# Batches 2 and 3 of the attention: two overlapped hand-written schedules replaced by one schedule per batch, with one load buffer instead of two

## The chip, the cores and the metric

One core of one Trainium2 chip. The time is the device time of the whole kernel in microseconds (us), one launch, median of several runs. The profile is one execution of the kernel, recorded by the hardware; its times count from the start of its span.

## What is computed

```python
def phi(x):                                   # per head: 8 x 8 products of two sketches
    a = einsum('rd,bhsd->bhsr', S1, x)
    b = einsum('rd,bhsd->bhsr', S2, x)
    return einsum('bhsi,bhsj->bhsij', a, b).reshape(..., 64)

q_p, k_p = phi(q), phi(k)                     # q, k, v: 4 batches, 4 heads, 1088 tokens, 32 wide
kv  = einsum('bhsf,bhsd->bhfd', k_p, v)
z   = sum(k_p, axis=2)
num = einsum('bhsf,bhfd->bhsd', q_p, kv)
den = einsum('bhsf,bhf->bhs', q_p, z)[..., None] + 1e-6
x   = (num / den) as (4352 tokens, 128)
out = ((1 / (1 + exp(-(x @ w_gate)))) * (x @ w_val)) @ w_out     # 128 -> 1536 -> 128
```

The weights and S1, S2 come in 64-bit floats, the rest in 32-bit floats.

## The kernel before, in words

Two pieces of work are interleaved by hand. The order of the instructions on TensorE, VectorE, ScalarE and GpSimd is the order in which the code emits them; only SyncE's queue of transfers is ordered by the framework.

**The feed-forward part is a row of slots.** The 4352 tokens are cut into eight chunks of 512 and one of 256, and the 1536 hidden columns into twelve groups of 128. A chunk has twelve slots (the last, of 256 tokens, has six); slot 0 to 11 are chunk 0, 12 to 23 chunk 1, 24 to 35 chunk 2, and so on to slot 101. In each slot `w1` emits the matmuls of one group into a PSUM tile `wave` (two buffers, line 542), ScalarE takes the sigmoid of one half (`sg`, line 550), and VectorE multiplies the halves into `g` (`glu`, line 585), which also frees the `wave` buffer for the slot after the next. In chunks 1 to 7 the product with `w_out` is done with seven instead of eight block products; GpSimd forms the sums of tokens for it (`tsum`, line 371), and TensorE's products (`prod`, line 381) come three and four slots after their `g`. The function `slot(group, n)` emits `group` first, then for each of n slots: `glu` of the slot before, waiting results, the products that have come due, and `w1`. `until(n)` runs plain slots up to slot n.

**The attention part of a batch is a chain of steps placed between slots.** For batch b:
- `load_kq(b)` transfers k and q (544 KB each) into one tile; `load_v(b)` transfers v. Both go through SyncE's queue.
- `turn_k`, `turn_q` (two halves): transposes on VectorE, lines 648 and 659.
- `begin(b)`: `kps`, sketches of k on TensorE (line 681) with two transposes on VectorE (`kab`, line 691), and `qcomp`, sketches of q on TensorE (line 827) into a `wave` buffer; ScalarE copies them out (`cq`, line 835) and `spread` writes them to DRAM and reads them back, repeated over partitions, into `qp`, `bq`, `a8` and `b8` (lines 852 and 874).
- `outer(b, 0)` and `outer(b, 1)` (line 760) and `sum_z(b, 0)`, `sum_z(b, 1)` (line 937): the features of k and their sum, on VectorE.
- `kv` (lines 903 and 912, 40 small matmuls, 80 records) and `kvd` (ScalarE, line 925): the product of the features with v.
- `ndt` (line 968, line 976) and `weights_z` (lines 1012 to 1019): small rearrangements of that product.
- `qmult(b, 0)`, `qmult(b, 1)` (line 881): the features of q, on VectorE, from `qp` and `bq`.
- `parts(b)`: denominators (`den_j` line 1032, `den_i` line 1045) and numerators (line 1271) on TensorE, then the division on VectorE, which writes the tokens of the batch into `xT`. A chunk may begin only when the tokens it reads have been written.

**Buffers.** Batches 0 and 1 load into the tile `kq` of the pool `ld`, of which there is one. The same memory serves as `bq` of each batch, so that a load waits until `qmult` of the batch before has read `bq`. Batches 2 and 3 load into a second tile, `kq2`, in a pool `late`, which takes the memory of the pool `sbN` (temporaries of the weight conversion) once that is closed. `kv` of batch 1 has a PSUM tile of its own; `kv` of batches 2 and 3 writes into unused columns of a tile of another step, that of `kps` of batch 3 and that of the numerators of batch 2.

**Order around the change.** Batch 1 is done at slots 12 to 23. Then, with `turn_k(2)` at slot 24: `begin(2)` at 27, features of batch 2 at 28, 29, 31 and 32; `turn_k(3)` at 34; `begin(3)` together with `kv(2)` at 36; `outer(3)` at 37 and 38, `ndt(2)` at 38, `qmult(2)` at 40 and 44, `sum_z(3)` at 41 and 42; `parts(2)` together with `kv(3)` at 45; `ndt(3)` at 48, `qmult(3)` at 50 and 52, `parts(3)` at 56. From slot 57 on no attention work is left.

Of the kernel before, what the change touches and what calls it, by code (L numbers as in the profile page):

```python
# [16 lines left out]
P = 128  # L17
# [3 lines left out]
def kernel(  # L21
# [31 lines left out]
    ld = ctx.enter_context(tc.tile_pool(name="ld", bufs=1))  # L53
    sbA = ctx.enter_context(tc.tile_pool(name="sbA", bufs=2))
    raw = ctx.enter_context(tc.tile_pool(name="raw", bufs=NJ // 2))
    sbG = ctx.enter_context(tc.tile_pool(name="sbG", bufs=3))
    top = ExitStack()
    sbN = top.enter_context(tc.tile_pool(name="sbN", bufs=1))

    dram = ctx.enter_context(tc.tile_pool(name="dram", bufs=1, space=bass.MemoryType.DRAM))  # L60

# [203 lines left out]
    k_t, q_t = {}, {}  # L265


    late_pool = []

    def new_kq(b):  # L270
        pool, tag, w = (ld, "kq", 2 * H * W1) if b < 2 else (late_pool[0], "kq2", 2 * T * D)
        t = pool.tile([P, w], F32, tag=tag, name="kq")
        kq = t[:, : 2 * T * D].rearrange("p (a t d) -> p a t d", a=2, t=T)
        k_t[b], q_t[b] = kq[:, 0], kq[:, 1]

# [390 lines left out]
    WD = 160  # L666
    mask = {}

    def kps(b, also=None):
        t = ps2.tile([P, 2, 512], F32, tag="two", name="kps")  # L670
        if also is not None:
            kv(also, ZS[also], t[:, 0, NJK * 32 : NJK * 32 + 2 * F])
        ts = [t[:, 0], t[:, 1]]
        turns = [(g, pi) for g in range(4) for pi in range(2)]

        if b == 0:
            ts[1] = pso.tile([P, TCH], F32, tag="acc1", name="kps1")
# [164 lines left out]
    def spread(b, ns, cq, put, get):  # L842
        p0 = 64 * ns[0]
        d = dram.tile([P, 2, W1], F32, tag="dq", name="dq")
        put.dma_start(out=d[p0:], in_=cq[p0:])
        for n in ns:
            for i, t in enumerate((QP[b], BQ[b])):

                for c in (0, 1) if i else (0,):
                    d0 = d[64 * n + 32 * c + 2 * i, 0]  # L850
                    rows = [[0, R], [8 * W1, R]] if i else [[8 * W1, 2 * R], [0, R]]
                    get.dma_start(
                        out=t[64 * c : 64 * c + 64 if i else P, n * H * W1 : (n + 1) * H * W1],
                        in_=bass.AP(
                            tensor=d0.tensor, offset=d0.offset, ap=rows + [[1, H * W1]]
                        ),
                    )
        if len(ns) < 2:
            return
        put = get  # L860

        pool = late_pool[0] if b == B - 1 else sbA
        B8[b] = pool.tile([P, W1], F32, tag="b8", name="b8", bufs=1)
        A8[b] = pool.tile([P, 2, WD], F32, tag="a8", name="a8", bufs=1)
        for x in range(2):
            for m in range(2):
                p0 = 64 * x + 32 * m
                for i, t in enumerate((A8[b], B8[b])):
                    d0 = d[2 * i + m, 0]
                    if i == 0:  # L870
                        offset, run = d0.offset + (W1 - WD) * x, [[W1, 2], [1, WD]]
                    else:
                        offset, run = d0.offset + W1 * x, [[1, W1]]
                    put.dma_start(
                        out=t[p0 : p0 + 32],
                        in_=bass.AP(tensor=d0.tensor, offset=offset, ap=[[8 * W1, 32]] + run),
                    )
# [16 lines left out]
                    skip_group_check=True,  # L894
                )

    def kv(b, zsum, kvz=None):
        if kvz is None:
            kvz = ps2.tile([P, 2, 512], F32, tag="two", name="kvz")[:, 0]
        KVZ[b] = kvz  # L900
        for j in [1, 2, 3, 4, 5, 6, 7, 8, 0]:
            for h in range(H):
                nc.tensor.matmul(  # L903
# [336 lines left out]
    slot(None, 1)  # L1240
    cq = {}

    def begin(b, also=None):
        glu()
        kps(b, also)
        if also is not None:
            moe["copies"].append(lambda: kvd(also))
        cq[b] = qcomp(b, (0, 1), (psm, "wave"))
        spread(b, (0, 1), cq[b], nc.scalar, nc.sync)

# [25 lines left out]
                    stop=True,  # L1276
                )

    def parts(b, also=None):
# [12 lines left out]
        turn_den(b, den_i(b, t[:, 0, :WD]))  # L1292
        if also is not None:
            moe["copies"].append(lambda: kvd(also))
# [64 lines left out]
    def until(n):  # L1359
        slot(None, n - moe["n"])  # L1360

    def features(b, *at):
        steps = [(outer, 0), (outer, 1), (sum_z, 0), (sum_z, 1)]
        for n, (step, i) in zip(at, steps):
            until(n)
            step(b, i)

    until(24)
    turn_k(2)
    until(25)  # L1370
    turn_q(2, 0)
    until(26)
    turn_q(2, 1)
    load_kq(3)
    until(27)
    slot(lambda: begin(2), 1)
    features(2, 28, 29, 31, 32)
    until(34)
    turn_k(3)
    until(35)  # L1380
    turn_q(3, 0)
    turn_q(3, 1)
    until(36)
    slot(lambda: begin(3, 2), 1)
    load_v(3)
    until(37)
    weights_z(2)
    outer(3, 0)
    until(38)
    slot(lambda: ndt(2), 1)  # L1390
    outer(3, 1)
    until(40)
    qmult(2, 0)
    until(41)
    sum_z(3, 0)
    until(42)
    sum_z(3, 1)
    until(44)
    qmult(2, 1)
    until(45)  # L1400
    slot(lambda: parts(2, 3), 1)
    until(48)
    weights_z(3)
    slot(lambda: ndt(3), 1)
    until(50)
    qmult(3, 0)
    until(52)
    qmult(3, 1)
    until(56)
    slot(lambda: parts(3), 1)  # L1410
    slot(None, 10**3)


# [28 lines left out]
```

## Time and profile before

| what | value |
|---|---|
| median of 3 runs | 294.0 us (293.81, 294.0, 297.79) |
| the profiled execution: its own time | 294.0 us |
| its span | 292.2 us, so 1.8 us lie around it |
| records of TensorE's matmuls | 2264 |
| matmuls into `wave` (line 542) | 820 records, 210.8 us busy |
| `prod` products (line 381) | 588 records, 169.2 us busy in four groups that overlap each other |
| `glu` products (line 585) | 96, 687 ns each |
| `tsum` (line 371) | 168, 779 and 831 ns on average, median about 730 ns |
| `kv`, per batch (lines 903, 912) | 80 records, 1.25 us from start to end |

A TensorE instruction is recorded with a modelled end, and matmuls on two halves of the array overlap, so busy times of groups add up to more than the engine's own. In a stretch without attention work, slots 60 to 71, twelve slots take 29.66 us (from 182.21 to 211.87 us in the chain of waits), 2.47 us each: 1.72 us for the matmuls of `w1` and, by turns, 0.65 and 0.86 us for the products with `w_out`.

### The profile page before, as it was taken

The page shows a single profiled execution, that of the slowest core. Times are in us where ns is not written, and L with a number is a line of the kernel's source. Part 1 is how long each engine was busy: PE and PEld are TensorE (multiplying, and loading weights), DVE is VectorE, ACT ScalarE, POOL GpSimd, SP SyncE. Part 2 cuts the span into 40 slices and gives each one's busy share as a digit, 9 for nine tenths or more (in the row PEclk, how much of TensorE's full clock was granted, in tenths as well). Part 3 has the DMA queues.
Part 4 walks back from the last instruction along what each step waited for, and adds up shares of the span by engine and source line. Part 5 has one row for each costly group of instructions (what it writes and reads, how often), then busy time and mean ns, then how long its engine had stood idle before and what let it go on. Part 6 is the DMA issues. An engine that isn't in the chain of part 4 may idle for free.

```text
span 292.2 us, 5780 instructions
## 1 busy us (share of the span) xinstructions
PE 286.1 (98%) x2264; PEld 159.8 (55%) x2264; DVE 174.6 (60%) x302; ACT 102.2 (35%) x207; POOL 158.9 (54%) x222
## 2 busy tenths in 40 slices
PE   8899999999999999999999999999999999999995
PEld 4444433355454555456565545555555555555895
DVE  6987889975877773797737474352235223522471
ACT  3676532322335222442325232342234222422341
POOL 2566556595544955468266644656555555656200
PEclk9999999999999999999999999999999999999999
DMA  7994434474425855462500200002000200020012
GB/s 215 340 354 117 115 136 170 131 173 102 93 35 208 202 128 118 121 139 48 146 8 1 38 2 1 0 4 34 1 0 2 36 2 0 0 38 0 3 15 41
DMA packets 28891, 24.24 MB, mean 83 GB/s; under 512 B 18560, under 2 KB 24064, under 8 KB 28864
## 3 DMA queue, kind: packets, MB, share of 16 engines
q1 hardware_dynamic: 25808, 21.95, 29.7%
q10 hardware_dynamic: 3056, 1.92, 2.3%
q8 instruction: 18, 0.29, 0.4%
q14 instruction: 9, 0.07, 0.1%
HBM read 20.60 MB, written 3.26 MB: 82 GB/s over the span
## 4 chain that ended last, share of the span: by engine, by line
PE 96%; POOL 1%; ACT 1%; DVE 1%; issue 0%; POOLq 0%
PE wave L542 60%; PE prod L381 21%; PE moeout L425 4%; PE warm L301 2%; PE moeout L451 2%; POOL tsum L371 1%; PE nps L1271 1%; PE kps L681 1%; PE cqps L827 1%; PE nps L1093 0%; PE denj L1032 0%; PE nps L1045 0%; PE dps L1074 0%; PE nps L903 0%; PE kvz L888 0%; PE kvz L903 0%
## 5 line engine op out<-in xcount | busy, mean ns | idle before, releaser
L542 PE MATMUL wave<-xT,w_sb 128*64 128x512 f32 (+3 forms) x820 | 210.8, 566 | 0.1
L542 PEld LDWEIGHTS wave<-xT,w_sb 128*64 128x64 f32 (+1 forms) x820 | 86.2, 140 | 62.4 <-issue 50.1
L550 ACT ACTIVATE sg<-wave 128x512 f32<-128x512 f32 x102 | 60.9, 598 | 163.6 <-PE wave L542 161.5
L585 DVE TENSOR_TENSOR g<-wave,sg 128x512 f32<-128x512 f32 x96 | 65.9, 687 | 81.6 <-ACT sg L550 81.4
L371 POOL TENSOR_TENSOR tsum<-g,tsum 128x256 f32<-128x256 f32 x84 | 69.8, 831 | 66.5 <-DVE g L585 66.2
L371 POOL TENSOR_TENSOR tsum<-g 128x256 f32<-128x256 f32 x84 | 65.5, 779 | 27.1 <-DVE g L585 26.9
L381 PE MATMUL prod<-tsum,ws 128*64 128x256 f32 x252 | 69.1, 381 | 0.7 <-POOL tsum L371 0.7
L381 PE MATMUL prod<-g,w_sb 128*64 128x256 f32 x168 | 50.1, 380 | 0.0
L381 PEld LDWEIGHTS prod<-tsum,ws 128*64 128x64 f32 x252 | 32.5, 137 | 10.4 <-issue 5.5
L381 PEld LDWEIGHTS prod<-g,w_sb 128*64 128x64 f32 x168 | 22.8, 137 | 22.8 <-issue 20.0
L381 PE MATMUL prod<-tsum,w_sb 128*64 128x256 f32 x84 | 25.0, 380 | 0.0
L381 PE MATMUL prod<-g,ws 128*64 128x256 f32 x84 | 25.0, 379 | 0.0
L118 POOL TENSOR_TENSOR head<-head,tail 128x384 int32<-128x384 int32 (+1 forms) x10 | 9.9, 988 | 13.7 <-DVE head L112 10.2
L381 PEld LDWEIGHTS prod<-g,ws 128*64 128x64 f32 x84 | 11.5, 137 | 3.4
L381 PEld LDWEIGHTS prod<-tsum,w_sb 128*64 128x64 f32 x84 | 11.4, 137 | 3.1 <-issue 2.1
L425 PE MATMUL moeout<-g,w_sb 128*128 128x512 f32 (+1 forms) x28 | 12.5, 603 | 0.0
L760 DVE TENSOR_TENSOR kp<-kab 128x1152 f32<-128x1152 f32 (+2 forms) x10 | 11.2, 1135 | 0.0
L881 DVE TENSOR_TENSOR qp<-qp,bq 128x1152 f32<-128x1152 f32 (+1 forms) x7 | 10.2, 1464 | 1.5 <-DMA bq<-dq 1.5
L578 DVE TENSOR_TENSOR g<-wave,sg 128x512 f32<-128x512 f32 x6 | 6.7, 1112 | 6.4 <-ACT sg L550 6.4
L492 DVE TENSOR_TENSOR res<-prod,other 128x256 f32<-128x256 f32 x14 | 5.9, 424 | 4.0 <-ACT other L483 2.2
L301 PE MATMUL warm<-const-float32-1.0 128*128 128x512 f32 (+2 forms) x12 | 7.2, 729 | 0.8 <-PEq L1426 0.8
L425 PEld LDWEIGHTS moeout<-g,w_sb 128*128 128x128 f32 (+1 forms) x28 | 4.1, 174 | 6.1 <-issue 3.7
(142 smaller groups left out, 200.3 us busy)
## 6 DMA issues: line engine op xcount, KB each, us to landing
qp<-dq SPq DMA_DIRECT2D x7, 576.0 KB, 5.0
bq<-dq SPq DMA_DIRECT2D x14, 288.0 KB
kq<-in_k_dram SPq DMA_DIRECT2D x3, 544.0 KB
kq<-in_q_dram SPq DMA_DIRECT2D x3, 544.0 KB
w_in<-in_moe_w_out_dram SPq DMA_DIRECT2D x6, 256.0 KB
w_in<-in_moe_w_gate_dram SPq DMA_DIRECT2D x5, 256.0 KB, 6.0
w_in<-in_moe_w_val_dram SPq DMA_DIRECT2D x5, 256.0 KB, 6.0
v<-in_v_dram SPq DMA_DIRECT2D x8, 144.0 KB
```

The source lines that it names most:

```text
L118: nc.gpsimd.tensor_tensor(out=head, in0=head, in1=tail, op=ALU.add)
L301: nc.tensor.matmul(out=t[:, 0, :n], lhsT=x, rhs=r, start=True, stop=True)
L371: nc.gpsimd.tensor_tensor(out=t[:, u], in0=in0, in1=in1, op=ALU.subtract)
L381: nc.tensor.matmul(out=out, lhsT=lhsT, rhs=rhs, start=start, stop=stop, skip_group_check=True)
L425: nc.tensor.matmul(out=moe["acc"][d], lhsT=w_sb[:, 2, j, d], rhs=g[:, jj], start=(j == 0), stop=(j == NJ - 1),)
L492: nc.vector.tensor_tensor(out=out, in0=in0, in1=in1, op=ALU.add)
L542: nc.tensor.matmul(out=wv[d, which, jj * tw + o : jj * tw + o + tp], lhsT=w_sb[:, which, j0 + jj, d], rhs=xT[:, t0 + o : t0 + o + tp], sta ...
L550: nc.scalar.activation(out=sg, in_=wv[:, 0], func=ACTF.Sigmoid)
L578: nc.vector.tensor_tensor(out=g.rearrange("p (j u s y) -> p j y u s", j=2, u=2, y=4), in0=wv[:, 1].rearrange("p (j y u s) -> p j y u s", j ...
L585: nc.vector.tensor_tensor(out=g, in0=wv[:, 1], in1=sg, op=MUL)
L760: eng.tensor_tensor(out=KP[b][:, pi, j0:j1].rearrange("p j m (i l) -> p (j m) i l", i=R), in0=bass.AP(tensor=a0.tensor, offset=a0.offset, ...
L881: nc.vector.tensor_tensor(out=q0, in0=q0, in1=half(BQ[b], n), op=MUL)
```

## The change

The pool `late` and the tile `kq2` go (`a8` and `b8` of batch 3, which lay there too, now share the tiles of the other batches). All four batches load into the one tile `kq`, and `sbN` keeps its memory to the end. `kv` of batches 2 and 3 becomes a step of its own with its own PSUM tile, as batch 1 has it (`kv_all`). The overlapped list of steps of batches 2 and 3 is replaced by one loop with the twelve slot numbers of each batch: batch 2 from slot 27 to 44, batch 3 from slot 48 to 68.

```diff
-    late_pool = []
-
     def new_kq(b):
-        pool, tag, w = (ld, "kq", 2 * H * W1) if b < 2 else (late_pool[0], "kq2", 2 * T * D)
-        t = pool.tile([P, w], F32, tag=tag, name="kq")
+        t = ld.tile([P, 2 * H * W1], F32, tag="kq", name="kq")
...
-    def kps(b, also=None):
+    def kps(b):
         t = ps2.tile([P, 2, 512], F32, tag="two", name="kps")
-        if also is not None:
-            kv(also, ZS[also], t[:, 0, NJK * 32 : NJK * 32 + 2 * F])
...
-        first = t
+        nc.scalar.copy(out=num, in_=t)
         t = ps2.tile([P, 2, 512], F32, tag="two", name="nps2")
         numerators(b, t[:, :, WD : WD + 32], True)
-        if also is not None:
-            kv(also, ZS[also], t[:, 1, 4 * F : 6 * F])
-        nc.scalar.copy(out=num, in_=first)
         turn_den(b, den_i(b, t[:, 0, :WD]))
-        if also is not None:
-            moe["copies"].append(lambda: kvd(also))
...
-    top.close()
-    late_pool.append(ctx.enter_context(tc.tile_pool(name="late", bufs=1)))
     slot(last01, 1)
     load_v(1)
-    load_kq(2)
     turn_k(1)
...
     qmult(1, 1)
+    load_kq(2)
     slot(None, 1)
     slot(lambda: parts(1), 1)
...
+    plan = {2: (27, 29, 30, 31, 32, 34, 36, 37, 38, 39, 42, 44)}
+    plan[3] = (48, 49, 51, 53, 56, 57, 58, 59, 60, 61, 63, 68)
+    for b in range(2, B):
+        at = iter(plan[b])
+        until(next(at))
+        turn_k(b)
+        for n in range(2):
+            until(next(at))
+            turn_q(b, n)
+        until(next(at))
+        slot(lambda: begin(b), 1)
+        for pi in range(2):
+            until(next(at))
+            outer(b, pi)
+        for step in range(2):
+            until(next(at))
+            sum_z(b, step)
+        until(next(at))
+        slot(lambda: kv_all(b), 1)
+        if b + 1 < B:
+            load_v(b + 1)
+        until(next(at))
+        qmult(b, 0)
+        slot(lambda: ndt(b), 1)
+        weights_z(b)
+        until(next(at))
+        qmult(b, 1)
+        load_kq(b + 1)
+        until(next(at))
+        slot(lambda: parts(b), 1)
     slot(None, 10**3)
```

The list that the loop replaces (`until(24)` to `parts(3)`) is left out here; its slot numbers stand above. On GpSimd the two kernels have the same instructions in the same order. On TensorE the same instructions stand in another order from the `begin` of batch 2 on, in the emitted program; on SyncE the load of batch 2 moves from behind that of batch 1 to behind the load of v of batch 2, and the load of batch 3 from ahead of `spread(2)` to behind the stores of chunk 2.

More of the change, by code (lines that the diff above doesn't have):

```diff
@@ L55 @@
     raw = ctx.enter_context(tc.tile_pool(name="raw", bufs=NJ // 2))
+    sbN = ctx.enter_context(tc.tile_pool(name="sbN", bufs=1))
     sbG = ctx.enter_context(tc.tile_pool(name="sbG", bufs=3))
-    top = ExitStack()
-    sbN = top.enter_context(tc.tile_pool(name="sbN", bufs=1))
     dram = ctx.enter_context(tc.tile_pool(name="dram", bufs=1, space=bass.MemoryType.DRAM))
@@ L860, in spread @@
         put = get
-        pool = late_pool[0] if b == B - 1 else sbA
-        B8[b] = pool.tile([P, W1], F32, tag="b8", name="b8", bufs=1)
-        A8[b] = pool.tile([P, 2, WD], F32, tag="a8", name="a8", bufs=1)
+        B8[b] = sbA.tile([P, W1], F32, tag="b8", name="b8", bufs=1)
+        A8[b] = sbA.tile([P, 2, WD], F32, tag="a8", name="a8", bufs=1)
         for x in range(2):
@@ L895, in kv0, with kv @@
                 )
[L897 to L900, printed above, removed]
+    def kv(b, zsum):
+        kvz = KVZ[b] = ps2.tile([P, 2, 512], F32, tag="two", name="kvz")[:, 0]
         for j in [1, 2, 3, 4, 5, 6, 7, 8, 0]:
@@ L1241, with begin @@
     cq = {}
-    def begin(b, also=None):
+    def begin(b):
         glu()
-        kps(b, also)
-        if also is not None:
-            moe["copies"].append(lambda: kvd(also))
+        kps(b)
         cq[b] = qcomp(b, (0, 1), (psm, "wave"))
@@ L1277, in numerators, with parts @@
                 )
-    def parts(b, also=None):
+    def parts(b):
         den_j(b)
@@ L1285, in parts @@
         num = num.rearrange("p c j m f -> p (c j m f)")[:, :1024].rearrange("p (c w) -> p c w", c=2)
-        first = t
+        nc.scalar.copy(out=num, in_=t)
         t = ps2.tile([P, 2, 512], F32, tag="two", name="nps2")
         numerators(b, t[:, :, WD : WD + 32], True)
-        if also is not None:
-            kv(also, ZS[also], t[:, 1, 4 * F : 6 * F])
-        nc.scalar.copy(out=num, in_=first)
         turn_den(b, den_i(b, t[:, 0, :WD]))
-        if also is not None:
-            moe["copies"].append(lambda: kvd(also))
         for n in range(2):
@@ L1360, in until @@
         slot(None, n - moe["n"])
[L1362 to L1410, printed above, removed]
+    plan = {2: (27, 29, 30, 31, 32, 34, 36, 37, 38, 39, 42, 44)}
[28 more added lines that the diff above has]
+        slot(lambda: parts(b), 1)
     slot(None, 10**3)
```

## The prediction

> **What bounds the kernel now.** I read the page's busy times and clock first, then what TensorE waited for, then the stretch that the change touches.
>
> ```profile
> PE 286.1 (98%) x2264; PEld 159.8 (55%) x2264; DVE 174.6 (60%) x302; ACT 102.2 (35%) x207; POOL 158.9 (54%) x222
> ...
> PEclk9999999999999999999999999999999999999999
> ```
> ```profile
> PE warm L301 <- PEq L1426: 0.8, 1, 0.8
> PE prod L381 <- POOL tsum L371: 0.7, 1, 0.7
> ```
> ```profile
> 57.00:146.00 89.00, 88.18 (x878) 47.70 (x876) 64.74 (x101) 27.68 (x54) 55.06 (x67) 1.00 0.54 128
> 146.00:176.00 30.00, 30.00 (x228) 16.58 (x226) 17.66 (x33) 10.19 (x21) 17.18 (x23) 1.00 0.08 13
> ```
> TensorE is busy for 286.1 of 292.2 us at full clock, and the longest two of its named waits are 0.8 and 0.7 us. The third view gives stretches: length, then busy time of TensorE, weight loads, VectorE, ScalarE, GpSimd, then clock, DMA share and GB/s. From 57 to 146 us, where batches 1 to 3 run, TensorE is idle for 89.00 - 88.18 = 0.82 us, of which 0.71 us is the wait for `tsum` at 58.4 us, slot 16, ahead of anything that the change reorders on TensorE. VectorE has 64.74 of 89 us of work there. So TensorE's list of matmuls is the time. The change can gain only what the present order wastes inside a busy TensorE, and lose only by making TensorE wait.
>
> **What the present order wastes.** A busy TensorE is not the same as a row of slots at 2.47 us. I count the excess over plain slots from the chain of waits. Slot 22 starts at 77.14 us and slot 58 at 177.21 us, both behind 0.86 us of products: 36 slots in 100.07 us, against 36 x 2.4717 (29.66 / 12) = 88.98 us. The attention steps of batches 2 and 3 on TensorE therefore cost 11.09 us. Batch 1 shows what the same steps cost in the form that the change gives to batches 2 and 3, each at its own place and at slots of the same parity (start, length, what):
>
> ```profile
> 61.19 1.72 PE wave L542 x8
> 62.91 1.14 PE kvz L903 x72
> 64.05 0.11 PE kvz L912 x8
> 64.16 1.01 PE prod L381 x8
> 65.17 1.72 PE wave L542 x8
> ```
> Slot 17 to slot 18 is 3.98 us with `kv` between them, against 2.58 us for such a pair (1.72 + 0.86): `kv` alone costs 1.40. From 65.17 to 87.09 us are eight slots, 21.92 - 19.77 = 2.15 us for `ndt` (0.22), `parts` (74.47 to 76.28, 1.81) and 0.12 of small change. `begin` alone, before slot 27, is 87.09 to 90.72 us, 3.63 less 2.42: 1.21. Sum for one batch: 1.40 + 2.15 + 1.21 = 4.76; for two, 9.52 us. The present order pays 11.09, so 1.57 us more than two copies of batch 1. Where this sits can be seen at two places:
>
> ```profile
> 110.50 1.93 PE wave L542 x8
> 112.43 1.14 PE kps L903 x72
> ...
> 114.82 1.01 PE prod L381 x8
> 115.83 1.72 PE wave L542 x8
> ```
> ```profile
> 141.49 0.64 PE prod L381 x5
> 142.12 1.51 PE wave L542 x6
> 143.63 0.12 issue
> ```
> The joint `kv` and `begin` takes 5.33 - 2.58 = 2.75, against 1.40 + 1.21 = 2.61 apart: 0.14. `ndt` of batch 2 (118.19 to 121.20, 3.01 - 2.58) costs 0.43 against 0.22: 0.21. `parts` with `kv` (136.65 to 142.12, less 2.37) costs 3.10 against 1.81 + 1.40: minus 0.11. The slot behind it (142.12 to 145.47) takes 3.35 in place of 2.58: 0.77, a real loss, while VectorE runs the division of batch 2. Those make 1.01 us; 0.56 of the 1.57 is not located. I take 1.1 us, nearer to what is located; 0 and 1.6 are the ends.
>
> **The change part by part.**
>
> *TensorE.* The same instructions in another order; `kv` stands alone twice, and no `parts` holds a `kv` ahead of `den_i`. Minus 1.1 us. `parts(2)` moves to slot 44 and `parts(3)` to 68, even slots as 22 and 56 are, where it cost 1.81 and 1.80 us (167.89 to 172.27, less 2.58); the slot behind slot 56 starts 2.36 us later, without the loss of 0.77.
>
> *VectorE and ScalarE.* Nothing is added; work of batch 3 moves from 106 to 175 us into about 145 to 205 us, where VectorE has 13.91 us of work in 30 (172 to 202). What matters is the `glu` that each step delays. In a plain slot the `glu` of slot 59 ends at 182.01 + 0.69 = 182.70 us, and its buffer is wanted by slot 61 at 184.52: 1.8 us of cover. The worst new neighbours are two `res` sums and `turn_k` ahead of a `glu` (0.42 + 0.42 + 1.30 = 2.14 us) and two `res` sums and `qmult` (0.42 + 0.42 + 1.21 to 1.74). The row nearest to them is in the trace: 0.42 + 0.42 and `outer` at 1.75 us before a `glu` at 124.54, with TensorE busy all the time. They cost 0; without that cover up to 0.4 us each (2.14 + 0.1 less 1.8), for some four places 1.6 us.
>
> *GpSimd.* Same list. Its `tsum` of about 0.73 us takes up to 2.05 us beside VectorE's `outer`, `sum_z` and `qmult`. The page "SBUF — State Buffer" of the Trainium skill, section "Who interferes with whom", says that VectorE and GpSimd share a pair of ports under an exclusive lock; by that rule the moved features of batch 3 would hold up `tsum` in chunk 4 instead of chunk 3, which is the same sum elsewhere. By the rows, GpSimd between 122 and 126 us was busy for 3.91 of 4 us beside such work without a wait on TensorE, and chunk 4 has VectorE less full. Cost 0.
>
> *The loads.* This is where the change adds waits. `load_kq(2)` now waits in SyncE's queue for `qmult(1, 1)`, which ends at 72.34 + 1.48 = 73.8 us, and for the v loads ahead of it, issued up to 74.5 us: k and q go out at about 75. `turn_k(2)` needs k at slot 27, about 88.5 us (slot 27 starts at 90.72 now, less the 1.21 of `begin`, less one us for the place of the step): 13.5 us. The trace has no landing for these loads, so bounds: batch 1's went out at 39.87 and 40.28 us, k was transposed at 46.45 and q at 48.24 with no wait for a DMA, so at most 6.6 and 8.0 us; from below, the 3.1 us of a 256 KB part. From the other side, `spread(1)` with 2.3 MB took from 54.43 to 72.34 us, 128 GB/s, at which 1.1 MB would take 8.7 us. All fit into 13.5. `load_kq(3)` waits for `qmult(2, 1)` at slot 42, about 131 us, and stands behind eight stores (0.73 us each to issue, 2.91 for four); `turn_k(3)` at slot 48 is about 146 us: some 9 us left behind the stores, again enough, with the least margin of the two. Behind a late `turn_k` on VectorE stands `glu`, and behind that TensorE.
> "Trainium Kernel Development and Optimization" of the Trainium skill, section "Best Practices", asks for double buffers so that transfers overlap compute; it speaks against going from two load tiles to one. By that rule each load would be exposed; by the rows both are still hidden under slots.
>
> *`spread`.* Its data came back for the first `qmult` 12.7 us after `cq` (51.62 to 64.3) and for the second after 20.7 (to 72.34), with VectorE waiting 0.21 and 1.29 us. The new distances are 8 slots and 11 (batch 2) or 10 (batch 3), with `kv` between: at least 21 and 26 us. Cost 0, cover 8 and 5 us.
>
> *Gates.* Chunk 4 needs batch 2 at slot 48 (`parts` at 44) and chunk 6 batch 3 at slot 72 (`parts` at 68). The division ended 5.5 us after `pd` (170.14 to 175.72), and four slots are 9.9 us. Cost 0.
>
> Sum: span 292.2 - 1.1 = 291.1 us; with the 1.8 us around it 292.9. The profiled execution's 294.0 us is the median of the runs too, so I predict 292.9 us.
>
> **The rivals.**
>
> *Hidden anyway, 0.25.* The 1.1 us are not tied to the order (0.56 were not located, and delays beside DMA or GpSimd may follow the work to its new place), or VectorE's neighbours give some back. Then 293.5 to 295, middle 294.2.
>
> *Slower by the single load tile, 0.20.* Place: `turn_k(2)` and `turn_k(3)`, VectorE blocked in front of `glu`. It decides once a load takes longer than its margin plus the 1.8 us of cover: about 15 us for batch 2 and 11 us, counted from behind the stores, for batch 3; from there every us is a us. For: every load now waits for the last reader of `bq`, and SyncE's queue stands still in front of it (the queue's own waits in batch 1: 2.5 us between single issues of `spread`). Against: the bounds of 6.6 and 8.7 us. At the 18 us of a `spread` for each, the price is 3 + 7 = 10 us less the 1.1: 303; half of that, 298. So 295 to 303.
>
> *TensorE not bound by its list:* a gain over 2% would need 5.9 us, and TensorE's idle time in the whole span is 292.2 - 286.1 = 6.1 us, nearly all at the start and the end. 0.01.
>
> **How the numbers follow.** The forecast has 0.54 (292.2 to 293.5, from the ends of 1.6 and the lower part of 0). The range from 292.2 to 296.5 takes it, the hidden case and the lower part of the slow one. 2%, about what a measurement of this kernel can tell from no change, is 5.9 us: 288.1 and 299.9. Faster 0.01; slower 0.08, the upper part of the slow case; the rest, 0.91, within 2%.
>
> **What would show it.** Right: TensorE's busy time near 285 to 286 us, idle 57 to 146 us no more than 0.8 us, the slot behind `parts(2)` back at about 2.4 to 2.6 us, `kv` at some 1.25 us as `kvz` three times, no `turn_k` or `qmult` waiting for a DMA over 1.8 us, `parts` ending before slots 48 and 72. Wrong: VectorE's `kT` waiting for a DMA with TensorE's `wave` or `prod` waiting for `glu` behind it, around 88 or 146 us; `tsum` late in chunk 4; or a chain that no longer runs through TensorE from 58 us on.

## The result and the profile after

| | before | after |
|---|---|---|
| median | 293.75 us (22 runs, 293.08 to 297.79) | 292.58 us (22 runs, 292.38 to 293.48) |
| ratio to before | | 0.9967, 95% interval 0.996 to 0.9974 |
| profiled execution, its span | 294.0, 292.2 us | 292.82, 291.0 us |

The change gains 0.3%, 1.2 us; 292.9 us and a span of 291.1 were forecast. One run of the kernel before, at 297.79 us, lies apart from the other 21 (293.08 to 294.24 us) and is not in the ratio. First the busy times on the page of the changed kernel, as they were shown of before, and the clock in the 40 slices of the span:

```profile
PE 284.9 (98%) x2264; PEld 158.3 (54%) x2264; DVE 173.9 (60%) x302; ACT 102.5 (35%) x207; POOL 158.6 (55%) x222
...
PEclk9999999999999999999999999999999999999999
```

The same 2264 records of matmuls at the same clock take 1.2 us less of a busy TensorE. Its longest two waits (total us, times, longest):

```profile
PE warm L297 <- PEq L1389: 0.8, 1, 0.8
PE prod L377 <- POOL tsum L367: 0.7, 1, 0.7
```

They are those of before. The two stretches (length, busy time of TensorE, weight loads, VectorE, ScalarE, GpSimd, then clock, DMA share, GB/s):

```profile
57.00:146.00 89.00, 88.29 (x790) 47.80 (x788) 56.25 (x92) 27.90 (x54) 53.04 (x71) 1.00 0.44 106
146.00:176.00 30.00, 30.00 (x208) 17.29 (x204) 19.31 (x29) 9.77 (x20) 19.98 (x23) 1.00 0.38 92
```

TensorE is idle for 0.71 us from 57 to 146 us, all of it the wait for `tsum` at slot 16. VectorE's work has moved on: 56.25 us in the first stretch (64.74 before), 19.31 in the second (17.66). Next the chain of waits at slot 38, where `kv` of batch 2 now stands alone, and then at slots 43 to 45 with `parts(2)` in 44 (start, length, what):

```profile
115.42 1.72 PE wave L538 x8
117.14 1.14 PE kvz L894 x72
118.28 0.11 PE kvz L903 x8
118.39 1.01 PE prod L377 x8
119.40 1.72 PE wave L538 x8
```
```profile
131.88 1.93 PE wave L538 x8
133.81 0.43 PE denj L1023 x16
134.24 0.95 PE nps L1260 x28
135.19 0.42 PE nps L1036 x4
135.61 0.86 PE prod L377 x8
136.48 1.72 PE wave L538 x8
138.19 0.64 PE prod L377 x5
138.83 1.72 PE wave L538 x8
140.56 0.86 PE prod L377 x6
```

`kv` takes 1.25 us, as forecast. The slot that held `parts(2)` runs to 136.48; the one behind it (136.48 to 138.83) takes 2.35 us and the next 2.59 (to the end of its `prod`, 140.56 + 0.86). The 3.35 us of before, with its piece of "issue", are gone.

The single load tile shows on SyncE's queue and on VectorE. Issues of the load of batch 3, then the transposes that read it:

```profile
132.55 0.44 SPq L241 DMA_DIRECT2D kq<-in_k_dram  x1
133.04 0.44 SPq L241 DMA_DIRECT2D kq<-in_q_dram  x1
```
```profile
144.10 0.69 DVE L581 TENSOR_TENSOR g<-wave,sg 128x512 f32<-128x512 f32 x1 [1.97 <-ACT sg L546]
144.71 1.30 DVE L644 STREAM_TRANSPOSE kT<-kq 128x1088 f32<-128x1088 f32 x1
```

The brackets give the idle time in front of an instruction and what ended it. `kT` has none: it starts where `g` ends, 12.2 us after the issue. For batch 2 the distance is 14.5 us (74.18 to 88.66), without a wait either.

**A finer measure.** Differences of 0.3 us are near the scatter of whole runs, and the start of the profiles varies by more (the sigmoid of slot 12 starts between 49.18 and 49.76 us). The experiments are therefore also read slot by slot: the length of slot n is the time from the start of the sigmoid of slot n - 1 to that of slot n, on ScalarE. Counted so, a step and the `w1` behind it are one slot, and the 0.77 us that the prediction found behind `parts(2)` lie in slot 45. Each kernel has one profile, but slots in which TensorE has the same work, such as 62 to 67, agree to 0.01 us in all of them. The stretch from the sigmoid of slot 13 to that of slot 72 holds all of the change; it takes 160.22 us before and 159.05 after, 1.17 less. These are some of the slots where the kernels differ, with four of the experiments told of below (lengths in us; the last row is the whole stretch):

```
slot    before  b_kv3_apart  b_bq_early  b_kv_apart  b_begin_35   after
34       2.60      2.60         2.60        4.00        4.00       2.60
35       2.51      2.50         2.51        2.57        3.84       2.51
36       5.13      5.13         5.13        3.88        2.60       2.60
37       2.56      2.56         2.56        2.56        2.19       2.19
38       2.98      2.98         2.99        2.81        2.81       3.99
39       2.63      2.63         2.63        2.46        2.57       2.85
44       2.60      4.00         2.60        4.00        4.00       4.40
45       6.44      4.36         5.70        4.36        4.36       2.56
13-72  160.22    159.55       159.62      159.40      159.01     159.05
```

### The profile page after: what moved, and what is told of

The parts are those of the page before. It is cut to its first block, busy times and chain, and to the rows that moved or that the text cites. A ratio compares the mean times of both kernels' runs of the same rounds, so it can differ in the third digit from the quotient of the medians.

```text
span 291.0 us, 5784 instructions
## 1 busy us (share of the span) xinstructions
PE 284.9 (98%) x2264; PEld 158.3 (54%) x2264; DVE 173.9 (60%) x302; ACT 102.5 (35%) x207; POOL 158.6 (55%) x222
## 4 chain that ended last, share of the span: by engine, by line
PE 96%; POOL 1%; ACT 1%; DVE 1%; issue 0%; POOLq 0%
PE wave L538 60%; PE prod L377 21%; PE moeout L421 4%; PE warm L297 2%; PE moeout L447 2%; POOL tsum L367 1%; PE kvz L894 1%; PE nps L1260 1%; PE kps L675 1%; PE cqps L821 1%; PE nps L1084 0%; PE denj L1023 0%; PE nps L1036 0%; PE dps L1065 0%; ACT asb L792 0%; PE kvz L881 0%
## 5 line engine op out<-in xcount | busy, mean ns | idle before, releaser
L367 POOL TENSOR_TENSOR tsum<-g,tsum 128x256 f32<-128x256 f32 x84 | 67.9, 808 | 62.0 <-DVE g L581 62.0
L367 POOL TENSOR_TENSOR tsum<-g 128x256 f32<-128x256 f32 x84 | 67.3, 802 | 30.3 <-DVE g L581 30.0
L377 PEld LDWEIGHTS prod<-g,ws 128*64 128x64 f32 x84 | 11.5, 137 | 3.5
L754 DVE TENSOR_TENSOR kp<-kab 128x1152 f32<-128x1152 f32 (+2 forms) x10 | 10.6, 1080 | 0.0
```

What stands on the lines that cost most here:

```text
L367: nc.gpsimd.tensor_tensor(out=t[:, u], in0=in0, in1=in1, op=ALU.subtract)
L377: nc.tensor.matmul(out=out, lhsT=lhsT, rhs=rhs, start=start, stop=stop, skip_group_check=True)
L754: eng.tensor_tensor(out=KP[b][:, pi, j0:j1].rearrange("p j m (i l) -> p (j m) i l", i=R), in0=bass.AP(tensor=a0.tensor, offset=a0.offset, ...
```

## The experiments

In the first group of kernels the code before is changed in one place each, to find where the 1.17 us come from; in the second, the changed kernel.

### kv(3) apart from parts(2) (b_kv3_apart)

```diff
     until(44)
+    slot(lambda: kv_all(3), 1)
     qmult(2, 1)
     until(45)
-    slot(lambda: parts(2, 3), 1)
+    slot(lambda: parts(2), 1)
```

> The kernel before, with one part of the change: kv of batch 3 is a step of its own at slot 44 instead of standing inside parts(2) at slot 45. Theory 1 (the 0.77 us behind parts(2) are lost because kv's 80 small matmuls stand in parts, ahead of den_i and of the copy of the numerators): slot 45 to 46 falls from 3.35 to about 2.6 us, the total by 0.7 us. Rival A (the odd slot, or the division on VectorE, makes the loss): slot 45 to 46 stays at 3.3 us and the total within 0.3 us. Rival B (the transfer of bq of batch 3, which runs from 137 to 147 us, makes it): it stays too, because that transfer is where it was.

293.15 us, ratio 0.9981 (0.9972 to 0.999); the stretch 159.55, 0.67 less than before. Slots 44 and 45 together take 8.36 us in place of 9.04. The chain of waits of this kernel around the place (start, length, what):

```profile
140.85 0.42 PE nps L1045 x4
141.27 0.64 PE prod L381 x5
141.91 1.72 PE wave L542 x8
143.64 0.86 PE prod L381 x6
```

The eight matmuls of `wave` take 1.72 us without a break, where before they were six, an "issue" of 0.12 and the rest. It looked as if `kv` inside `parts` were the cause. The next two runs say no.

### parts(2) with kv(3) at an even slot (b_parts_44); qmult(2, 1) earlier (b_bq_early)

```diff
-    until(44)
+    until(43)
     qmult(2, 1)
-    until(45)
+    until(44)
     slot(lambda: parts(2, 3), 1)
```

> The kernel before, with parts(2), kv(3) still inside, one slot earlier: at slot 44 instead of 45, and qmult(2, 1) at 43 instead of 44, so that the transfer of bq of batch 3 moves along. Theory 1 (kv inside parts) and rival B (the transfer beside it): the slot behind parts(2) stays at 0.7 to 0.8 us over its plain length, the total within 0.2 us of the kernel before. Rival A (an odd slot): the loss goes, the total falls by 0.7 us.

```diff
     until(41)
-    sum_z(3, 0)
+    qmult(2, 1)
     until(42)
+    sum_z(3, 0)
+    until(43)
     sum_z(3, 1)
-    until(44)
-    qmult(2, 1)
     until(45)
```

> The kernel before, with qmult(2, 1) at slot 41 instead of 44 and sum_z of batch 3 at 42 and 43 instead of 41 and 42, so that the transfer of bq of batch 3 starts some 8 us sooner and is over, or nearly, when parts(2) with kv(3) runs. Theory 1 and rival A: the slot behind parts(2) keeps its loss of 0.77 us. Rival B (the transfer): the loss falls to 0.2 us or less and the total by 0.6 us.

The first gives 293.02 us, 0.9966 (0.9943 to 0.9989), stretch 159.46; the second 293.15, 0.997 (0.9946 to 0.9995), stretch 159.62. In both `kv` is still inside `parts`, in the second at the same slot 45 as before, with the same division behind it on VectorE. Yet the slot takes 5.70 us in place of 6.44 (5.73 at slot 44). So neither the joint step, nor its slot, nor the division is the cause. Nor is the transfer of `bq` beside it enough by itself: in `b_parts_44` it runs beside the step as before. One profile stands for each kernel, but the medians agree: these three are 0.66 to 0.79 us below the 293.81 of the kernel before, run with them.

What is common to these kernels is when TensorE's instructions arrive. On the page of before, among the DMA queues (packets, MB, share of 16 engines):

```profile
q8 instruction: 18, 0.29, 0.4%
```

That is 18 packets of 16 KB. One comes for about every 256 records of matmuls and weight loads: in the changed kernel the eighth, ninth and tenth start at records 1980, 2246 and 2471, before at 1970, 2475 and 2513. The ninth, read from the trace's packets (us; a record is a matmul or a weight load, counted in the order of their starts; "2240" is the time at which the 2240th starts, taken, from the 2246 of the changed kernel, as about the point at which this piece is due):

```
                 2240    piece starts   lands    record at landing   slot with or behind parts(2)
before          138.48      141.30      142.46        2493           6.44, 0.71 of it stopped
b_outer_later   140.20      142.70      143.65        2487           5.84, told of below
b_bq_early      138.40      139.34      140.77        2462           5.70, no stop
b_parts_44      136.85      137.51      138.47        2439           5.73, no stop
b_kv3_apart     135.85      136.56      137.52        2353           no stop
b_begin_35      135.22      136.06      137.24        2357           no stop
after           136.74      137.23      138.19        2254           no stop
```

Before, the piece starts 2.8 us late and lands when TensorE is at record 2493. At record 2497, a piece's worth (256) behind 2240, all starts of TensorE cease from 143.04 to 143.75 us. The weight loads of before show it (idle time and what ended it in brackets):

```profile
141.75 0.57 PEld L542 LDWEIGHTS wave<-xT,w_sb 128*64 128x64 f32 x4
142.61 0.14 PEld L542 LDWEIGHTS wave<-xT,w_sb 128*64 128x64 f32 x1 [0.29 <-issue]
143.75 0.13 PEld L542 LDWEIGHTS wave<-xT,w_sb 128*64 128x64 f32 x1 [1.00 <-issue]
143.76 0.13 PEld L381 LDWEIGHTS prod<-tsum,ws 128*64 128x64 f32 x1
```

"<-issue" after 1.00 us of idle is the mark: the profile shows no semaphore and no data that it waited for, and the next four loads start within 0.07 us, as if they had all been ready. Shorter idle times with this mark, as the 0.29, stand everywhere. What is rare is that matmuls and weight loads both stop: between 57 and 215 us of before, only this hole and the wait for `tsum` are longer than 0.55 us. No other kernel here has a hole that long without a semaphore. The theory from here on is that TensorE ran out of instructions.

### kv of both batches apart (b_kv_apart)

```diff
+    slot(lambda: kv_all(2), 1)
+    load_v(3)
     turn_k(3)
...
-    slot(lambda: begin(3, 2), 1)
-    load_v(3)
+    slot(lambda: begin(3), 1)
...
+    slot(lambda: kv_all(3), 1)
     qmult(2, 1)
     until(45)
-    slot(lambda: parts(2, 3), 1)
+    slot(lambda: parts(2), 1)
```

> The kernel before, with both kv apart: kv(2) at slot 34 on its own instead of at begin(3) in slot 36, kv(3) at slot 44 on its own. The places of the other steps and the two load tiles stay. If kv inside other steps is all of the gain: 1.0 to 1.2 us below the kernel before, at the changed kernel's 292.6. If the spreading of the steps over slots 27 to 68 makes it: within 0.3 us of the kernel before. In between if theory 1 holds for slot 45 alone: 0.7 to 0.9 us.

293.15 us, 0.9973 (0.9949 to 0.9996), stretch 159.40: 0.15 less than with `kv(3)` alone apart. The table of slots says why it is so little. At slots 34 to 37 this kernel takes 13.01 us where before took 12.80, so the joint `kv` and `begin` was the cheaper form, by 0.21. What it gains, 0.34, lies at slots 38 and 39 (5.27 for 5.61). VectorE of before shows the loss there:

```profile
118.50 0.23 DVE L1012 TENSOR_TENSOR zz<-kvd,unit 128x64 f32<-128x64 f32 x1 [3.21 <-ACT kvd L925]
118.76 0.22 DVE L1018 TENSOR_REDUCE z<-zz 128x8 f32<-128x64 f32 x1
119.01 0.22 DVE L1019 TENSOR_TENSOR zw<-z,eight 128x64 f32<-128x64 f32 x1
119.15 1.35 DVE L760 TENSOR_TENSOR kp<-kab 128x1152 f32<-128x1152 f32 x1
120.42 0.68 DVE L585 TENSOR_TENSOR g<-wave,sg 128x512 f32<-128x512 f32 x1
```

`weights_z(2)` waits 3.21 us for the copy of `kv`, `outer` stands behind it, and the `glu` behind both comes late: TensorE's next weight load for `wave` is held up by it for 0.41 us:

```profile
121.16 0.20 PEld L542 LDWEIGHTS wave<-xT,w_sb 128*64 128x64 f32 x4 [0.41 <-DVE g L585]
```

### The pieces of instructions shifted (b_shift_page); outer later (b_outer_later)

32 matmuls of 64 columns, of no use to the output, are put into slot 40. They leave everything around slot 45 in its place and shift the boundaries of the pieces by 128 records or so.

```diff
     until(40)
+    spare = ps2.tile([P, 2, 512], F32, tag="two", name="spare")
+    for x in range(32):
+        nc.tensor.matmul(out=spare[...], lhsT=w_sb[...], rhs=w_sb[:, 0, 0, :64], ...)
     qmult(2, 0)
```

> The kernel before, with 32 small matmuls (64 columns, of no use to the output) added at slot 40; nothing else differs: kv(3) inside parts(2) at slot 45 and the transfer of bq of batch 3 beside it. New theory: TensorE's instructions come in pieces of 16 KB through the same DMA engines (18 such packets in the trace); in the kernel before, the piece that slot 45 needs is queued behind that transfer and lands at 142.46 us, when TensorE has used up what it holds, and it starts again at 143.75. The added matmuls are 128 instructions, half a piece, so the piece is asked for before the transfer begins: sigmoid 44 to sigmoid 45 falls from 6.44 to about 5.7 us, while slot 40 gets about 1.1 us longer; total 0.2 to 0.5 us above the kernel before. Rival (something in that slot itself, such as kv's place, the odd slot or VectorE's division): 6.44 stays, and the total is 1.0 to 1.2 us above.

294.34 us, 1.0017 (1.0007 to 1.0027), stretch 160.5. Slots 40 to 43 take 11.07 us where they took 10.05, the price of the matmuls, and slot 45 takes 5.68 in place of 6.44: with more work ahead of it, the loss is gone. The ninth piece starts at 129.76 us, 11.5 us earlier.

```diff
     weights_z(2)
-    outer(3, 0)
     until(38)
     slot(lambda: ndt(2), 1)
-    outer(3, 1)
+    outer(3, 0)
     until(40)
-    qmult(2, 0)
+    outer(3, 1)
...
+    until(43)
+    qmult(2, 0)
     until(44)
```

> The kernel before, with outer(3, 0) and outer(3, 1) at slots 39 and 40 instead of 37 and 38, and qmult(2, 0) at 43 instead of 40. Theory: 0.2 to 0.4 us of the gain come from slot 37 to 38, where weights_z(2) waits 3.2 us on VectorE for kvd(2), outer(3, 0) follows it, and the glu behind both is late for TensorE's slot 38. Then sigmoid 37 to 38 falls from 2.98 to about 2.7 us, and with slot 45 at 6.44 the total falls by 0.2 to 0.4 us; if the moved steps also change what the piece of instructions meets, by up to 1.0. Rival (the ndt matmuls make it): 2.98 stays.

295.12 us, 1.0043 (1.003 to 1.0057), stretch 161.39: slower. The part that was asked for came: without `outer` behind `weights_z`, slots 38 and 39 take 2.81 and 2.46 us, 0.34 less than before, as with `kv(2)` apart. But with `qmult(2, 0)` moved to slot 43, just ahead of `qmult(2, 1)`, GpSimd is held up. GpSimd, then TensorE in this kernel:

```profile
133.53 3.44 POOL L371 TENSOR_TENSOR tsum<-g,tsum 128x256 f32<-128x256 f32 x1 [1.02 <-DVE g L585]
136.94 0.72 POOL L371 TENSOR_TENSOR tsum<-g 128x256 f32<-128x256 f32 x1
```
```profile
137.03 0.43 PE L381 MATMUL prod<-tsum,ws 128*64 128x256 f32 x1 [1.22 <-POOL tsum L371]
```

One sum takes 3.44 us beside two `qmult` (133.31 and 135.05 us on VectorE, with a `glu` between) and 0.72 when they are over. TensorE waits 1.22 us for it, and slot 44 takes 4.59 us in place of 2.60. This kernel is also a second witness for the late piece. It is the only other one in which the ninth piece starts more than 1 us late (2.5), and in both the same weight load, behind record 2497, is the first to come late. It starts at 144.86 us here, 1.2 us after the landing, and at 143.75 before, 1.3 us after. Here the piece lands some 0.5 us earlier against TensorE's place, and slot 45 takes 5.84, 0.14 above the 5.70 without a late piece, where before it was 0.74.

### Where begin(3) stands (b_begin_odd, b_begin_35)

0.35 us of stretch still separated the kernel with both `kv` apart from the changed one. The first kernel has `begin(3)` at slot 37 in place of 36. The edits are against the kernel before; the one that sets `kv(3)` apart, shown above, is left out in both.

```diff
+    until(33)
+    turn_k(3)
     until(34)
-    turn_k(3)
-    until(35)
+    slot(lambda: kv_all(2), 1)
+    load_v(3)
     turn_q(3, 0)
+    until(36)
     turn_q(3, 1)
-    until(36)
-    slot(lambda: begin(3, 2), 1)
-    load_v(3)
+    weights_z(2)
     until(37)
-    weights_z(2)
+    slot(lambda: begin(3), 1)
     outer(3, 0)
...
```

> The kernel before with both kv apart (slots 34 and 44) and begin(3) at the odd slot 37 instead of the even 36, its transposes at slots 33 to 36 and weights_z(2) ahead of it; two load tiles and the overlap of batches 2 and 3 stay. Theory: what is left between the kernel with both kv apart and the changed kernel is that begin at an even slot makes the slot behind it 0.37 us longer (slots 36 and 37: 1.28 + 0.37 over plain length; at odd slots 27, 31 and 53: 1.27 to 1.33 in all). Then slots 37 and 38 together are some 0.3 us shorter, and from sigmoid 13 to sigmoid 72 it takes 159.1 us as in the changed kernel (159.05), against 159.40 with both kv apart. Rival (the spreading of batch 3 over slots 48 to 68 is what is left): 159.4 stays.

292.98 us, 0.997 (0.9955 to 0.9986), stretch 159.40: not a hundredth better than with `begin(3)` at 36. Slots 36 and 37 take 6.44 us either way (3.88 + 2.56 or 2.60 + 3.84). The idea that odd and even slots differ falls. The lengths suggested another one: some slots last only 2.19 us (25, 29, 33, 37 and 41 of the changed kernel), and a `begin` in such a slot or just ahead of it takes that shortness away. So `begin(3)` goes to slot 35:

```diff
+    until(33)
+    turn_k(3)
     until(34)
-    turn_k(3)
+    turn_q(3, 0)
+    slot(lambda: kv_all(2), 1)
+    load_v(3)
+    turn_q(3, 1)
     until(35)
-    turn_q(3, 0)
-    turn_q(3, 1)
-    until(36)
-    slot(lambda: begin(3, 2), 1)
-    load_v(3)
+    slot(lambda: begin(3), 1)
...
```

> The kernel before with kv(2) and kv(3) as steps of their own, as in the run with both apart, and begin(3) one slot earlier, at 35 in place of 36 (the transposes of batch 3 at 33 and 34). What is asked: the 0.35 us between the run with both apart (159.40 us from slot 13 to slot 72) and the changed kernel (159.05). Theory: in the plain row two slots in every chunk or so last 2.19 us in place of 2.5 to 2.6 (25, 29, 33, 37, 41), and a step just ahead of such a slot takes its shortness away: with begin at 36, slot 37 lasts 2.56 us. With begin at 35 slot 35 should last 3.84 us, slot 36 2.60 and slot 37 2.19, and slots 13 to 72 159.07 us, the median about 292.7 us. Rival: begin(3) costs 1.65 us wherever it stands among the copies and sums of batch 2, and the 0.35 us come from the later chunks: then 159.4 us and about 293.0 again. If it is 159.07, the changed kernel has nothing left that this one has not, and the loop over batches itself brings nothing.

292.81 us, 0.9968 (0.9958 to 0.9979), stretch 159.01: slots 35, 36 and 37 take 3.84, 2.60 and 2.19 us, to the hundredth as expected, and the kernel is level with the changed one (159.05). With it the whole gain can be had in the old, overlapped schedule with two load tiles.

### The loads of the changed kernel (a_turn_early)

```diff
-    plan = {2: (27, 29, 30, 31, 32, 34, 36, 37, 38, 39, 42, 44)}
-    plan[3] = (48, 49, 51, 53, 56, 57, 58, 59, 60, 61, 63, 68)
+    plan = {2: (24, 25, 26, 31, 32, 34, 36, 37, 38, 39, 42, 44)}
+    plan[3] = (45, 46, 47, 53, 56, 57, 58, 59, 60, 61, 63, 68)
```

> The changed kernel, with the transposes of batch 2 at slots 24, 25, 26 instead of 27, 29, 30 and of batch 3 at 45, 46, 47 instead of 48, 49, 51, which leaves the loads into the one tile 6 to 7 us from their issue instead of 13 to 14. If a load takes 5 us, as the DMA rows let one think (traffic ends 5 us behind the issue at 74.2 and at 132.6 us): no wait of VectorE for kq, total within 0.3 us of 292.6. If a load takes 9 us: VectorE waits about 2 us in front of glu, twice, and 0.5 to 2 us are lost.

293.38 us, 0.9989 (0.998 to 0.9998), stretch 159.79. The transposes of batch 3 come five us earlier; VectorE there:

```profile
139.44 0.22 DVE L1294 TENSOR_TENSOR xT<-nps,rb 128x64 f32<-128x64 f32 x1
139.57 1.30 DVE L644 STREAM_TRANSPOSE kT<-kq 128x1088 f32<-128x1088 f32 x1
140.80 0.65 DVE L581 TENSOR_TENSOR g<-wave,sg 128x512 f32<-128x512 f32 x1
```

`kT` follows the division at 139.57 us, 7.3 us after its load went out at 132.28, and waits for no DMA. So k takes at most 7.3 us against the 12.2 that it has; q, issued at 132.77 us and transposed from 141.37, takes at most 8.6. The 0.74 us that this kernel loses on the changed one are at slots 46 and 47 (2.96 and 2.57 for 2.60 and 2.19): division and transposes together make `glu` late, and TensorE waits for its `g`:

```profile
141.50 0.20 PEld L538 LDWEIGHTS wave<-xT,w_sb 128*64 128x64 f32 x4 [0.60 <-DVE g L581]
```

### The wait for tsum at slot 16 (a_batch1_later, a_outer11_later)

The one wait for data left in the middle of the kernel, 0.71 us at slot 16, stands ahead of the change. Two edits of the changed kernel are aimed at it:

```diff
     slot(None, 1, behind=lambda: begin(1))
+    slot(None, 1)
     for pi in range(2):
...
-    slot(None, 1)
     qmult(1, 1)
```

> The changed kernel, with the features of batch 1 (outer, sum_z, kv, ndt) one slot later and qmult(1, 1) in the slot of ndt; parts(1) stays. It tries for a version better than both. In both kernels slot 16 waits 0.71 us for tsum, whose subtractions take 1.71 and 1.76 us beside outer and sum_z of batch 1. If VectorE's work there is the cause, the wait goes and sigmoid 15 to 16 falls from 3.93 to about 3.0 us: 0.7 to 1.0 us below the changed kernel. If the late glu of slot 13 or the start of the row of slots is the cause: no gain beyond 0.2 us.

```diff
-    for pi in range(2):
-        outer(1, pi)
-        slot(None, 1)
+    outer(1, 0)
+    slot(None, 2)
+    outer(1, 1)
+    slot(None, 1)
...
-    slot(None, 1)
     qmult(1, 1)
```

> The changed kernel, with outer(1, 0) where it is and outer(1, 1), sum_z(1), kv(1) and ndt(1) one slot later. Second try for a version better than both: the first tsum in line, 54.8 and 56.6 us, took 1.71 and 1.76 us beside outer(1, 1) and sum_z(1, 0); here VectorE has only glu beside them. If that overlap is what makes TensorE's 0.71 us at slot 16, they take 0.73 us each, the wait goes, and sigmoid 15 to 16 falls from 3.93 to about 3.2 us: 0.5 to 0.8 us below the changed kernel, unless the later steps of batch 1 give it back. If not, no change beyond 0.2 us.

The first gives 292.99 us, 0.9986 (0.9956 to 1.0016), stretch 159.2: no gain. The features of batch 1 still stand beside the first sums, which take 1.71, 1.90 and 1.77 us, and TensorE waits 0.8 us. The second removes the wait. GpSimd in the changed kernel, then GpSimd and one `outer` on VectorE in this one:

```profile
54.81 1.72 POOL L367 TENSOR_TENSOR tsum<-g,tsum 128x256 f32<-128x256 f32 x1 [3.19 <-DVE g L581]
56.47 1.77 POOL L367 TENSOR_TENSOR tsum<-g 128x256 f32<-128x256 f32 x1
58.20 0.73 POOL L367 TENSOR_TENSOR tsum<-g,tsum 128x256 f32<-128x256 f32 x1
```
```profile
54.51 0.73 POOL L367 TENSOR_TENSOR tsum<-g,tsum 128x256 f32<-128x256 f32 x1 [3.19 <-DVE g L581]
55.20 0.73 POOL L367 TENSOR_TENSOR tsum<-g 128x256 f32<-128x256 f32 x1
55.88 0.72 POOL L367 TENSOR_TENSOR tsum<-g,tsum 128x256 f32<-128x256 f32 x1
```
```profile
56.01 1.82 DVE L754 TENSOR_TENSOR kp<-kab 128x1152 f32<-128x1152 f32 x1
```

In the changed kernel `outer(1, 1)` and `sum_z(1, 0)` start at 54.58 and 56.44 us, just ahead of the two long sums. Here the first two sums have neither beside them and take 0.73 us. The third starts 0.13 us ahead of `outer(1, 1)` and keeps its 0.72 us; it is `outer` that takes 1.82 us in place of 1.35. Slot 16 takes 2.57 us in place of 3.93. Still the kernel takes 293.15 us, 0.9977 (0.9958 to 0.9997), stretch 159.57. TensorE's longest wait in it is a new one:

```profile
PE denj L1023 <- DMA b<-dq: 0.8, 2, 0.5
```

Slots 22, 23 and 24 take 5.86, 3.68 and 1.48 us in place of 4.39, 2.76 and 2.41. TensorE comes to `parts(1)` sooner, but the last part of `b8` of batch 1 goes out later, at 72.73 us (71.88 in the changed kernel). What was gained at slot 16 was given back at slot 22, and half a microsecond more.

### parts at odd slots in the changed kernel (a_parts_odd)

```diff
-    plan = {2: (27, 29, 30, 31, 32, 34, 36, 37, 38, 39, 42, 44)}
-    plan[3] = (48, 49, 51, 53, 56, 57, 58, 59, 60, 61, 63, 68)
+    plan = {2: (27, 29, 30, 31, 32, 34, 36, 37, 38, 39, 42, 45)}
+    plan[3] = (48, 49, 51, 53, 56, 57, 58, 59, 60, 61, 63, 69)
```

> The changed kernel, with parts(2) at slot 45 instead of 44 and parts(3) at 69 instead of 68. The prediction set the places of parts at even slots beside the costs of 1.8 us. If the parity of parts matters, the two slots of each parts together get 0.2 us or more longer; if not, total within 0.2 us of 292.6. Chunk 4 is gated by parts(2): its division, 5.5 us, must end before slot 48; if it does not, 1 us or more is lost there.

292.97 us, 0.9983 (0.9963 to 1.0004), stretch 159.50. Slots 44 and 45 take 6.96 us in both kernels (2.60 + 4.36 or 4.40 + 2.56), and so do 68 and 69: the slot of `parts` costs nothing. The 0.45 us more of its profile lie at slots 22 to 24 (10.02 us in place of 9.56), where the code is the same and `parts(1)` waits for the arrival of `spread(1)`. Profiles of the same code differ there: slots 22 and 23 take 4.39 + 2.76 us in the changed kernel, 4.40 + 2.57 in `a_turn_early` and 4.85 + 3.25 here.

## Why the prediction held, and where it did not

**The bound and the size.** TensorE's list of matmuls was the time and still is. The term of the sum was minus 1.1 us, the stretch shows minus 1.17, and the span fell by 1.2. Of the signs of being right, the busy time is 284.9 us (285 to 286 were forecast), the idle time from 57 to 146 us is 0.71 (at most 0.8), `kv` is 1.25 us three times, and no transpose waits for its load. One `qmult` does wait for a DMA longer than the 1.8 us named, 2.35 us at 66.5 us; it belongs to batch 1, and slots 17 to 21 are as long as before.

**The terms inside the 1.1 us.** Against before, the kernel `b_begin_35` differs by 1.21 us: 0.68 at slots 44 and 45, 0.23 at 38 to 41, 0.17 at 34 to 37 and 0.13 at 42 and 43. Set beside the prediction's list:

- *"The slot behind it ... 0.77, a real loss, while VectorE runs the division of batch 2"*, less 0.11 for the joint `parts` and `kv`: 0.66 forecast, 0.68 measured. The 0.77 itself measured 0.74, the 0.11 only 0.06 (5.70 us against 1.40 + 1.85 on top of a plain 2.51). But the surroundings named for the 0.77 were wrong: with the same division and the same joint step in the same slot it vanishes when `qmult` and its transfer, or the pieces of instructions, are shifted. This is the step of the prediction that failed, in its reason and not in its size. The row that gave it away stood in the prediction's own quotation, "issue" inside a run of `wave`. The loss belonged to no step of the order, and four quite different edits took it away: `kv` apart, the step a slot earlier, `qmult` earlier, useless matmuls ahead of it. That the new order is free of it is luck as far as the prediction goes: some 0.7 of the 1.17 us came because no piece of instructions stopped TensorE in the changed kernel, and nothing in the prediction said that it would not. Its rival "Hidden anyway" named the risk.
- *`ndt`, 0.21:* 0.23 measured. The cause, which was not named, is `weights_z` waiting on VectorE in front of `outer` and `glu`. It is 0.34 at slots 38 and 39, and 0.10 of that comes back at slot 41 in `b_kv_apart` (2.29 for 2.19).
- *Joint `kv` and `begin`, 0.14:* 0.17 measured, but not because they were joint. At the same slot for `begin` the joint form is the cheaper one by 0.21; what is dear is `begin` at slot 36, just ahead of a short slot, by 0.38.
- *0.56 not located:* the 0.13 at slots 42 and 43 are all of it that showed, and they stay unexplained. Some 0.40 was never there to gain: by the prediction's own count the two batches cost 11.09 - 1.17 = 9.92 us in the new order, not 9.52. `begin` for instance takes 1.27 to 1.33 us there (slots 31 and 53), not 1.21. Taking 1.1 rather than 1.6 was right in size.
- *Even slots for `parts`.* Irrelevant, as the odd slots of the changed kernel show.

What makes a `begin` in or just ahead of a short slot take its shortness is not known; only that it does was shown, with `begin` at 35, 36 and 37.

**The loads.** Batch 2 has 14.5 us (13.5 were reckoned) and batch 3 has 12.2 (9), and at most 7.3 (k) and 8.6 (q) are needed. The rival with exposed loads was decided by the bounds that the prediction took from batch 1, and the rule of the Trainium skill, "Trainium Kernel Development and Optimization", section "Best Practices", does not bite here: one tile, refilled 12 us ahead, is enough.

**VectorE and GpSimd at nothing.** True for this plan, not in general. Two kernels that pack VectorE a little closer wait on TensorE for 0.60 us (transposes behind a division) and 1.22 us (two `qmult` beside one `tsum`), and their slots get 0.74 and 1.99 us longer. The 0.4 us that the prediction set for one such place was too small for both.

**What stays open.** That the ninth piece was late, and that TensorE stopped a piece's worth of records behind the point at which it is normally asked for, is read from the packets in two kernels, one with a long and one with a short effect, and was removed at will with the useless matmuls. Why it started late is not settled. In both kernels the piece became due while the transfer of `bq` of batch 3 ran, 0.6 us after its first large packet in before and 2.4 us after it in `b_outer_later`. But `b_parts_44`, due 0.5 us after it, got its piece in 0.66 us, and `b_bq_early`, due 7.6 us after it, in 0.94. No kernel was run with that transfer alone taken away.

## What to carry to other kernels

When TensorE starts neither matmuls nor weight loads for longer than anywhere else in a run of like instructions, and the profile says "issue", with no semaphore behind it, suspect the arrival of instructions: look for the instruction packet that landed last before it, and test by adding or moving work that changes nothing else. Compare a plain row of slots by their single lengths, not by their mean, before pricing a step: where `begin` stands in the pattern changed its price here from 1.3 to 1.65 us. The wait removed at slot 16 was given back at slot 22, so ask what arrives at the next gate before spending effort on such a wait.

## What the runs showed of the hardware

- TensorE's instructions come in packets of 16 KB, about one for every 256 records, and one that started 2.8 us late stopped TensorE for 0.71 us; new instructions ran 1.2 to 1.3 us after the packet landed. The Trainium skill, "Runtime: NRT & Kernel Launch", section "Instruction fetch mechanics", describes this streaming in 16 KiB blocks of 256 instructions and calls its cost mostly hidden. The packets here agree with the size; that it is hidden holds, between 57 and 215 us of before, for all pieces but one.
- `tsum` on GpSimd: 0.73 us alone, 1.7 to 1.8 when it starts just behind one of VectorE's `outer` or `sum_z`, and 3.44 beside two `qmult`; where it started 0.13 us ahead of an `outer`, it kept 0.72 us and the `outer` took 1.82 in place of 1.35. These lengths look like the exclusive port lock of the Trainium skill, "SBUF — State Buffer", section "Who interferes with whom", which the prediction weighed against the trace. With little slack left they do reach TensorE (1.22 us).
